# A memory-bound decode kernel: the small q-weight load moved to the front, and the engines' programs emitted without a block

## The chip, the cores and the metric

The kernel runs on one core of one Trainium2 chip. The metric is the device time of one execution in microseconds (us). Each execution also has a *span*, from the first to the last instruction that the profile shows on the core. The device time is longer than the span by 1.2 to 2.1 us in the runs here, and that difference is a main character of this study. It is called "the time outside the span" below.

## The reference, cut to what matters

One decode step of a transformer layer, batch 4, one token each, model width 576, all inputs bf16:

```python
x  = A_x                                        # [4, 1, 576]
h  = x + attention(layernorm(x))                # 32 query heads, 16 kv heads, head size 128
h2 = h + (relu(hn @ W_gate) * (hn @ W_up)) @ W_down   # hn = layernorm(h), inner width 4608
# attention:
q = x @ wq                                      # wq: [576, 4096], 4.7 MB
k = k_cache[:, :, -4096:, :]                    # the last 4096 positions: 67 MB
v = v_cache[:, :, -4096:, :]                    # 67 MB
o = softmax(q @ k.T * 128**-0.5) @ v;  return o @ wo
```

The caches and weights make 159.58 MB to be read once; the output is 4.6 KB.

## The kernel before

The program is first written as a list of operations for each engine, with the operations that each waits for. `emit` turns that into instructions and semaphore waits. Before, this happens inside a block: each engine's program is a body of its own, and when the block closes, all engines meet at a barrier (in the profile before, SP waits 0.2 us there for PE's sequencer).

```python
# in Prog.emit
        block = es.enter_context(nc.Block())

        def run(engine, e):
            seen = {}
            for o in self.q[e]:
                ...                              # waits on semaphores, then the instruction
        for e in ENGS:
            getattr(block, e)(lambda engine, e=e: run(engine, e))
```

All large loads are issued by SP on one queue, in the order of this code. The weights with 576 rows are loaded in two parts: rows 0 to 511 with four rows (32 KB) on each of the 128 partitions, and the last 64 rows with half a row (4 KB) on each.

```python
        s = ring_slot()                          # one of four 4 MB slots
        place(("wq", 0), wq_off, TILE, "QMM",    # 4 MB: rows 0..511
              lambda e: e.dma_start(out=arena[:, wq_off:wq_off + TILE], in_=main_rows(A_wq)), key=f"slot{s}")
        P.dma("sync", ("L", "wq", 1), lambda e: e.dma_start(out=pT[:, 0:2048], in_=last_rows(A_wq)), "d_wq1")   # 0.5 MB
        for g in range(NTILE):                   # 16 K tiles and 16 V tiles of 4 MB
            add_kv("K", g)
            if g >= 4:
                add_kv("V", g - 4)
        ...                                      # wo, W_gate, W_up, W_down
            for r0, r1 in ((0, 9),) if j < 3 else ((0, 6), (6, 8), (8, 9)):   # the last W_down load is cut in three
```

The tensor engine multiplies with the main q rows first and with the last 64 rows at the end. Each K tile is transposed by DVE before the tensor engine uses it. The end of the program:

```python
        for n in range(2):                       # the output, one half from SP, one from ACT
            P.dma(("sync", "scalar")[n], ("O", n), ..., "d_out", [f"OUT{n}"])
        P.op("sync", None, None, [("O", n) for n in range(2)])    # SP waits for both
        P.emit(nc, es)
```

## Time and profile before

| what | value | seen in |
|---|---|---|
| device time, first three runs | 379.36, 380.56, 380.57 us | times |
| span of the profiled run | 378.6 us | page |
| its device time less its span | 380.66 - 378.6 = 2.1 us | times and page |
| HBM bytes | 159.58 MB | page |
| load queue's share of the 16 DMA engines' time | 98.3% | page, part 3 |
| PE, DVE busy | 56%, 60% | page, part 1 |

The page of the kernel before: the span, each engine's busy time, then busy tenths of the DMA engines and GB/s in forty slices of the span, and the load queue with its packets, MB and share.

```profile
span 378.6 us, 2587 instructions
...
PE 213.2 (56%) x1471; PEld 37.6 (10%) x703; DVE 225.6 (60%) x164; ACT 54.4 (14%) x85; POOL 10.6 (3%) x29
...
DMA  8999999999999999999999999999999999999994
GB/s 333 440 443 429 409 435 443 443 429 409 435 443 440 427 414 433 443 436 426 419 435 443 429 426 426 435 433 436 429 422 435 436 429 429 448 413 421 418 423 183
...
q1 hardware_dynamic: 6632, 159.59, 98.3%
```

Only the first and the last slice have slack: the kernel is one long stream. By the packet records of this trace, from the first load packet (1.84 us) to the end of the last (374.64) it is 159.58 MB in 372.80 us, 428 GB/s. (A single slice shows up to 448, because the view counts a whole packet in the slice in which it starts; with each packet's bytes spread over its duration, the same records give 423 to 433 in every slice but the first and the last.)

The start, from the timeline (start in us, duration in us, engine, line, operation; in brackets the engine's idle time before it and what ended that). SPq is the issue of a DMA by SP.

```profile
0.80 0.40 SPq L256 DMA_DIRECT2D sb_arena<-in_A_wq_dram  x1
1.26 0.41 SPq L257 DMA_DIRECT2D sb_pp<-in_A_wq_dram  x1
...
13.28 0.62 PE L384 MATMUL psb<-sb_arena,sb_xnT 128*32 128x512 bf16 x4 [4.68 <-DMA sb_arena<-in_A_wq_dram]
...
24.24 8.71 DVE L427 STREAM_TRANSPOSE sb_arena<-sb_arena 128x8192 f32<-128x8192 f32 x1 [2.29 <-DMA sb_arena<-in_A_k_cache_dram]
...
33.00 0.65 PE L451 MATMUL psb<-sb_arena 128*32 128x512 bf16 x4 [12.46 <-DVE sb_arena L427]
```

The q matmuls wait for their load until 13.28, the first K tile is there at 24.24, and the first QK matmul follows at 33.00.

The tensor engine at the end (two batches of W_down matmuls), and then what SP waited for last:

```profile
371.93 1.28 PE L707 MATMUL psb<-sb_arena,sb_pp 128*32 128x288 bf16 x18 [1.83 <-DMA sb_arena<-in_B_W_down_dram]
373.98 2.35 PE L707 MATMUL psb<-sb_arena,sb_pp 128*32 128x288 bf16 x18 [0.77 <-DMA sb_arena<-in_B_W_down_dram]
```

```profile
SPq L136 <- DMA out_dram<-sb_out_sb: 1.0, 1, 1.0
...
SPq L136 <- PEq L136: 0.2, 1, 0.2
```

Eighteen matmuls took 1.28 us, and eighteen equal ones 2.35. Line 136 is where the block closes: SP waits 1.0 us for the output, then 0.2 for the barrier.

### The profile page before, as it was taken

To read this page: it belongs to the slowest core of one execution; us is meant where nothing else is said; L and a number is where in the kernel's file an instruction comes from. 1 tells how busy PE (TensorE), PEld (TensorE's weight loads), DVE (VectorE), ACT (ScalarE), POOL (GpSimd) and SP (SyncE) were. 2 spreads that over 40 slices of the span, in tenths; PEclk is the share of its full clock that TensorE was granted. 3 is DMA by queue.
4 is the path that set the end of the run, shared out by engine and by line. 5 is a ranking of instruction groups with operands and counts; after the bars stand their busy time and mean duration, and the time that the engine had idled before them with its cause. 6 is when DMAs were issued, how large, how long until landed. Compare 5 with 4: busy or idle time off the path is not lost.

```text
span 378.6 us, 2587 instructions
## 1 busy us (share of the span) xinstructions
PE 213.2 (56%) x1471; PEld 37.6 (10%) x703; DVE 225.6 (60%) x164; ACT 54.4 (14%) x85; POOL 10.6 (3%) x29
## 2 busy tenths in 40 slices
PE   0404442239919091749292835573746697885764
PEld 0000000001001010101010100010100011002422
DVE  3178878779392959593848777666658513334120
ACT  3192000211010114010101140101010501113010
POOL 8200000000000000000000000000000000000000
PEclk9966866659969788697888796989686978998697
DMA  8999999999999999999999999999999999999994
GB/s 333 440 443 429 409 435 443 443 429 409 435 443 440 427 414 433 443 436 426 419 435 443 429 426 426 435 433 436 429 422 435 436 429 429 448 413 421 418 423 183
DMA packets 6659, 159.74 MB, mean 422 GB/s; under 512 B 749, under 2 KB 889, under 8 KB 1529
## 3 DMA queue, kind: packets, MB, share of 16 engines
q1 hardware_dynamic: 6632, 159.59, 98.3%
q8 instruction: 8, 0.13, 0.1%
q14 instruction: 3, 0.02, 0.0%
q10 hardware_dynamic: 16, 0.01, 0.0%
HBM read 159.58 MB, written 0.00 MB: 422 GB/s over the span
## 4 chain that ended last, share of the span: by engine, by line
DMA 56%; PE 22%; DVE 20%; issue 0%; SPq 0%; ACT 0%
DMA sb_arena<-in_A_k_cache_dram 48%; DVE sb_arena L427 16%; PE psb L34 13%; DMA sb_arena<-in_B_W_down_dram 8%; PE psb L451 4%; PE psb L512 3%; DVE sb_o_tmp L525 1%; DVE sb_pp L490 1%; PE psb L707 1%; PE psb L478 1%; DVE sb_pp L473 0%; DVE sb_hx L456 0%; ACT sb_pp L470 0%; SPq L286 0%; DVE sb_out_sb L710 0%
## 5 line engine op out<-in xcount | busy, mean ns | idle before, releaser
L427 DVE STREAM_TRANSPOSE sb_arena<-sb_arena 128x8192 f32<-128x8192 f32 (+1 forms) x19 | 139.9, 7365 | 67.5 <-DMA sb_arena<-in_A_k_cache_dram 67.5
L451 PE MATMUL psb<-sb_arena 128*32 128x512 bf16 x256 | 41.8, 627 | 120.3 <-DVE sb_arena L427 120.3
L34 PE MATMUL psb<-sb_arena,sb_pp 128*128 128x512 bf16 x384 | 108.3, 392 | 0.0
L512 PE MATMUL psb<-sb_arena,sb_pp 128*128 128x512 bf16 x128 | 50.9, 398 | 8.9 <-DVE sb_o_tmp L525 8.9
L522 ACT COPY sb_o_tmp<-psb 32x512 f32<-32x512 f32 x32 | 18.5, 578 | 181.4 <-PE psb L34 181.1
L34 PE MATMUL psb<-sb_arena 128*32 128x512 bf16 x256 | 43.4, 645 | 0.0
L525 DVE TENSOR_TENSOR sb_o_tmp<-psb,sb_fm 32x512 f32<-32x512 f32 x32 | 21.7, 678 | 18.6 <-PE psb L34 18.1
L451 PEld LDWEIGHTS psb<-sb_arena 128*32 128x32 bf16 x256 | 9.1, 119 | 162.9 <-DVE sb_arena L427 133.3
L512 PEld LDWEIGHTS psb<-sb_arena,sb_pp 128*128 128x128 bf16 x128 | 12.8, 100 | 116.6 <-issue 116.6
L529 DVE TENSOR_REDUCE sb_o_sel<-sb_o_tmp 128x128 f32<-128x512 f32 x16 | 17.7, 1105 | 0.5
L470 ACT ACTIVATE sb_pp<-psb,sb_hx 128x1024 bf16<-128x1024 f32 x4 | 4.5, 1114 | 80.7 <-DVE sb_hx L467 80.7
L490 DVE TENSOR_TENSOR sb_pp<-psb,sb_m 128x1024 bf16<-128x1024 f32 x8 | 9.3, 1207 | 4.8 <-PE psb L478 4.8
L485 ACT ACTIVATE sb_pp<-psb,sb_m 128x512 bf16<-128x512 f32 x16 | 9.7, 693 | 14.9 <-PE psb L478 14.9
L528 DVE TENSOR_TENSOR sb_o_tmp<-sb_o_tmp,sb_fm 64x512 f32<-64x512 f32 x16 | 11.0, 689 | 0.5
L418 ACT COPY sb_arena<-sb_q_keep 32x256 bf16<-32x256 bf16 x8 | 9.7, 1449 | 0.1
L707 PE MATMUL psb<-sb_arena,sb_pp 128*32 128x288 bf16 x72 | 6.2, 327 | 4.0 <-DMA sb_arena<-in_B_W_down_dram 4.0
L473 DVE STREAM_TRANSPOSE sb_pp<-sb_pp 128x1024 bf16<-128x1024 bf16 x4 | 5.0, 1245 | 5.1 <-ACT sb_pp L470 5.1
L478 PE MATMUL psb<-sb_pp,sb_to_v 128*32 128x256 bf16 x64 | 4.3, 401 | 6.3 <-DVE sb_pp L473 6.3
L404 DVE CAST sb_pp<-psb 128x512 bf16<-128x512 f32 x1 | 2.4, 2427 | 8.8 <-PE psb L384 8.8
L710 DVE CAST sb_out_sb<-psb 32x288 bf16<-32x288 f32 x1 | 0.4, 446 | 10.7 <-PE psb L707 10.7
L34 PE MATMUL psb<-sb_arena,sb_hnT 128*32 128x384 bf16 x80 | 6.4, 405 | 0.0
L456 DVE TENSOR_REDUCE sb_hx<-psb 128x1 f32<-128x1024 f32 x4 | 4.9, 1225 | 2.0 <-PE psb L34 2.0
(123 smaller groups left out, 81.2 us busy)
## 6 DMA issues: line engine op xcount, KB each, us to landing
sb_arena<-in_A_k_cache_dram SPq DMA_DIRECT2D x16, 4096.0 KB, 26.2
sb_arena<-in_A_v_cache_dram SPq DMA_DIRECT2D x16, 4096.0 KB, 28.5
sb_arena<-in_A_wo_dram SPq DMA_DIRECT2D x1, 4608.0 KB, 25.0
sb_arena<-in_B_W_gate_dram SPq DMA_DIRECT2D x1, 4608.0 KB, 26.5
sb_arena<-in_A_wq_dram SPq DMA_DIRECT2D x1, 4096.0 KB, 12.4
sb_arena<-in_B_W_down_dram SPq DMA_DIRECT2D x3, 1296.0 KB, 30.6
sb_arena<-in_B_W_up_dram SPq DMA_DIRECT2D x1, 3456.0 KB, 27.5
sb_arena<-in_B_W_up_dram SPq DMA_DIRECT2D x1, 1152.0 KB, 29.9
```

Of the source, the lines that this page charges most:

```text
L34: return e.add_instruction(mybir.InstMatmult(name=e.bass.get_next_instruction_name(), engine=mybir.EngineType.PE, ins=[e.lower_ap(rhs), e. ...
L418: act("QW", lambda e, i=i, q=q: e.copy(out=bass.AP(tensor=arena, offset=32 * i * AW + 2 * i + q, ap=[[AW, 32], [512, 16], [136, 4], [32, 4]]),
L427: dve(("TRA", g), lambda e: e.transpose(out=dst, in_=src), [("L", "K", g)] if lo == 0 else [])
L451: fn = lambda e, out_=out_, lhsT=lhsT, rhs=rhs, start=start, stop=stop: e.matmul(out_, lhsT=lhsT, rhs=rhs, start=start, stop=stop, skip_gr ...
L485: act(("EV", b, 0), lambda e, a=a: e.activation(out=bass.AP(tensor=pp, offset=2 * a, ap=[[PPW, 128], [8, 2], [32, 128], [1, 2]]), in_=bank ...
L490: dve(("EV", b, 1), lambda e, n=n: e.tensor_tensor(out=bass.AP(tensor=pp, offset=16 + 8 * n, ap=[[PPW, 128], [32, 128], [2, 4], [1, 2]]), ...
L512: fn = lambda e, lhsT=lhsT, rhs=rhs, k=k, j=j: e.matmul(bank[2 + j], lhsT=lhsT, rhs=rhs, start=(k == 0), stop=(k == 7), skip_group_check=True)
L522: act(("OSC", g), lambda e, j=j: e.copy(out=o_tmp[32 * j:32 * j + 32, 0:512], in_=bank[2 + j][32 * j:32 * j + 32, :]), [("PV", g), ("OSEL" ...
L525: dve(("OSD", g), lambda e, j=j: e.tensor_tensor(out=ot(32 * j, 32), in0=bank[2 + j][32 * j:32 * j + 32, :].rearrange("p (t d) -> p t d", ...
L528: dve(("OS", g), lambda e: e.tensor_tensor(out=ot(64, 64), in0=ot(64, 64), in1=fmb(64, 64), op=ALU.mult), [("OSC", g)])
L529: dve(("OSEL", g), lambda e: e.tensor_reduce(out=o_sel[:, qd, b, :], in_=o_tmp[:, 0:512].rearrange("p (t d) -> p d t", d=DH), axis=AX.X, o ...
L707: pe(("DOWN", n), lambda e, j=j, r=r, n=n, wv=wv: e.matmul(bank[n][32 * n:32 * n + 32, 0:288], lhsT=hhT[:, r * 128 + 32 * j:r * 128 + 32 * ...
```

## The change

Its intent: drop the block with its branches and closing barrier, since SP alone waits for the output and the engines need not meet; and put the small load of q weights in front, so that it is there when the main one lands.

```diff
-        block = es.enter_context(nc.Block())
-
...
         for e in ENGS:
-            getattr(block, e)(lambda engine, e=e: run(engine, e))
+            run(getattr(nc, e), e)
...
+        P.dma("sync", ("L", "wq", 1), lambda e: e.dma_start(out=pT[:, 0:2048], in_=last_rows(A_wq)), "d_wq1")
         s = ring_slot()
         wq_off = slot0 + s * TILE
         place(("wq", 0), wq_off, TILE, "QMM", ...)
-        P.dma("sync", ("L", "wq", 1), lambda e: e.dma_start(out=pT[:, 0:2048], in_=last_rows(A_wq)), "d_wq1")
```

## The prediction

> **What bounds the kernel now.** The input stream from HBM. The page counts 159.58 MB read in a 378.6 us span; the DMA engines are at 90% or more in every slice but the first and the last, and the load queue alone has 98.3% of their time. The first DMA is issued at 0.80, bytes move from about 1.8, and the last W_down piece lands at 373.98 (chain of waits): about 429 GB/s. [...] PE is 56% busy, DVE 60%; neither paces the middle. After the last landing comes a serial tail of 4.6 us: 18 W_down matmuls 2.35, the copy 0.45, the output's issue 0.34, its landing about 1.0 (SP's wait), and about 0.4 to the end of the span, of which 0.2 is SP's wait for PE's sequencer where the block closes.
>
> **What the change removes, adds, moves.**
> 1. The closing barrier: the last 0.2 to 0.4 us of the span, all on the chain. The wait for the output stays. I take away 0.3 us.
> 2. The block's entry. The constructor's barrier stays (SP waits 0.7 us there); the first DMA follows at most 0.1 us later. I take 0.05 us, on the chain because it shifts the stream.
> 3. The last 64 rows of the q weights (0.5 MB) go before the main 4 MB. Same bytes, queue and issue cost (0.40 and 0.41 us). At 0.43 MB per us the small piece takes 1.2 us: it lands near 4 us instead of 14.5, the main part near 14.5 instead of 13.28. PE used the small piece only at 16.67 and never waited for it; now the first q matmul starts 1.2 us later. The q chain, whose eight copies end at 30.9, ends near 32.1. The first QK matmuls start at 33.0 behind the first K transpose, which waits for K's landing at 24.2 and does not move. So the delay is swallowed, with 0.9 us left. The fourth K load waits for the q matmuls and is issued near 19 instead of 18, with some 10 MB still queued ahead: no gap in the stream.
>
> So of the 1.2 us shift nothing reaches the end, and some 0.35 us of barrier and entry do.
>
> **Prediction.** The runs before are 379.36, 380.56 and 380.57. I predict 379.9 us, range 378.7 to 380.9. Chances: faster by over 2% 0.01, within 2% 0.98, slower 0.01.
>
> **What would show it.** SP's last wait for PE's sequencer gone; the span's end 0.3 us or less after the output lands; first DMA issued at 0.7 to 0.8; small q piece landing near 4, first q matmul near 14.5; first K transpose still near 24.2, first QK matmul near 33.0; last W_down landing within 0.3 us of 373.9.
>
> **What would make it wrong.** (a) The last 18 matmuls ran at a granted clock of 0.50 and took 2.35 us, against 1.28 for as many at 1.00: another phase of the throttle moves the end by 1 us, more than the change. (b) The stream's rate varies by fractions of a per cent between runs, as large as the gain. (c) If the q copies end after the first K transpose, QK starts late, but the backlog absorbs it (loads land 26 us after issue, and take under 10). (d) Small first packets could start the stream earlier or later by tenths.

## More of the kernel before

All executions counted here are of the state "fast". Inside that state most kernels here have two modes about 1 us apart; they are called *short* and *long*, and what goes with them is one of the findings. Effects of a few tenths of a microsecond are compared between short runs alone.

## The result

The median of six runs is 377.93 us (377.82 to 378.96), beside 379.69 us for the kernel before (379.36 to 380.57, six runs). The ratio is 0.9956, with a 95% interval of 0.9938 to 0.9974. Ratios here are the mean time of one kernel's fast runs over that of the other's of the same rounds, so not quite the ratio of the medians quoted.

So the change is 1.7 us faster by the means (1.8 by the medians). It stays inside the 2% band, as forecast, but the time lies under the stated range, and the gain is some four to five times the 0.35 us that the prediction added up.

The page of the changed kernel, the same lines as above:

```profile
span 376.6 us, 2561 instructions
...
PE 208.2 (55%) x1456; PEld 38.0 (10%) x703; DVE 226.6 (60%) x164; ACT 54.3 (14%) x85; POOL 10.5 (3%) x29
...
DMA  8999999999999999999999999999999999999996
GB/s 335 446 446 425 409 446 446 425 418 439 444 421 428 429 444 428 421 432 446 428 423 428 446 425 432 420 446 425 435 421 446 423 432 425 442 419 422 435 415 259
...
q1 hardware_dynamic: 6632, 159.59, 98.8%
```

The span is 2.0 us shorter, but the device time of the same two executions differs by 380.66 - 377.82 = 2.84. The rest is outside the span: 377.82 - 376.6 = 1.2 us now, 2.1 before.

The start of the changed kernel:

```profile
0.80 0.40 SPq L251 DMA_DIRECT2D sb_pp<-in_A_wq_dram  x1
...
1.25 0.41 SPq L255 DMA_DIRECT2D sb_arena<-in_A_wq_dram  x1
...
14.12 0.62 PE L382 MATMUL psb<-sb_arena,sb_xnT 128*32 128x512 bf16 x4 [6.47 <-DMA sb_arena<-in_A_wq_dram]
...
23.80 8.71 DVE L425 STREAM_TRANSPOSE sb_arena<-sb_arena 128x8192 f32<-128x8192 f32 x1 [1.69 <-DMA sb_arena<-in_A_k_cache_dram]
...
32.56 0.66 PE L449 MATMUL psb<-sb_arena 128*32 128x512 bf16 x4 [11.86 <-DVE sb_arena L425]
```

The first issue has not moved (0.80), so leaving the block's entry away is worth nothing. But the first K tile is there 0.44 us earlier, although the same bytes go ahead of it. That size is of this pair of profiles: a second profile of the changed kernel (e15 below) has the transpose at 24.17, only 0.07 earlier. By the packet records, the stream now lasts 372.16 us from its first packet to its last, not 372.80. This is steadier: of the eleven kept profiles with the half megabyte in front and no pause, ten have 372.00 to 372.31 us (one, e11, 372.64); the three in the order of before (before, e2, e8) have 372.69 to 372.80.

The end of it, and SP's last waits:

```profile
371.27 1.28 PE L705 MATMUL psb<-sb_arena,sb_pp 128*32 128x288 bf16 x18 [1.82 <-DMA sb_arena<-in_B_W_down_dram]
373.32 1.37 PE L705 MATMUL psb<-sb_arena,sb_pp 128*32 128x288 bf16 x18 [0.77 <-DMA sb_arena<-in_B_W_down_dram]
```

```profile
SPq L110 <- DMA out_dram<-sb_out_sb: 1.0, 1, 1.0
SPq L730 <- PEq L730: 0.7, 1, 0.7
```

The barrier wait is gone (the line with 0.7 is the one at the program's start, which stays). The last eighteen matmuls took 1.37 us here and 2.35 there. That is the difference between the modes, not the change, as the runs show ("beside the experiments" means run in the same rounds):

| | short runs | long runs |
|---|---|---|
| before (44 runs beside the experiments) | 30, mean 379.48 | 14, mean 380.44 |
| changed (12 runs: the six above, and e15) | 7, mean 377.89 | 5, mean 378.88 |

The profile of before happened to be a long run and that of the changed kernel a short one. Of the 18 kept profiles three are long runs (before, e4, e5), and in just these three the clock of the last matmuls was 0.50; in the others it was 1.00. Between short runs the change is worth 379.48 - 377.89 = 1.59 us; it is this that the experiments have to explain.

### The profile page after: what moved, and what is told of

It is laid out like the page before. It is cut to its first block, busy times and chain, and to the rows that moved or that the text cites. A ratio compares the mean times of both kernels' runs of the same rounds, so it can differ in the third digit from the quotient of the medians.

```text
span 376.6 us, 2561 instructions
## 1 busy us (share of the span) xinstructions
PE 208.2 (55%) x1456; PEld 38.0 (10%) x703; DVE 226.6 (60%) x164; ACT 54.3 (14%) x85; POOL 10.5 (3%) x29
## 4 chain that ended last, share of the span: by engine, by line
DMA 56%; PE 22%; DVE 20%; issue 1%; SPq 0%; ACT 0%
DMA sb_arena<-in_A_k_cache_dram 48%; DVE sb_arena L425 16%; PE psb L34 13%; DMA sb_arena<-in_B_W_down_dram 9%; PE psb L449 4%; PE psb L510 3%; DVE sb_o_tmp L523 1%; DVE sb_pp L488 1%; PE psb L476 1%; PE psb L705 0%; DVE sb_pp L471 0%; DVE sb_hx L454 0%; ACT sb_pp L468 0%; SPq L284 0%; DVE sb_out_sb L708 0%
## 5 line engine op out<-in xcount | busy, mean ns | idle before, releaser
L449 PE MATMUL psb<-sb_arena 128*32 128x512 bf16 x256 | 44.6, 639 | 119.3 <-DVE sb_arena L425 119.3
L34 PE MATMUL psb<-sb_arena,sb_pp 128*128 128x512 bf16 x382 | 106.9, 388 | 2.8 <-issue 2.7
L510 PE MATMUL psb<-sb_arena,sb_pp 128*128 128x512 bf16 x115 | 44.8, 390 | 8.9 <-DVE sb_o_tmp L523 8.9
L34 PE MATMUL psb<-sb_arena 128*32 128x512 bf16 x256 | 45.5, 646 | 0.0
L449 PEld LDWEIGHTS psb<-sb_arena 128*32 128x32 bf16 x256 | 10.0, 118 | 162.0 <-DVE sb_arena L425 132.4
L705 PE MATMUL psb<-sb_arena,sb_pp 128*32 128x288 bf16 x72 | 5.2, 288 | 4.0 <-DMA sb_arena<-in_B_W_down_dram 4.0
```

The lines of the kernel that those rows point to most:

```text
L34: return e.add_instruction(mybir.InstMatmult(name=e.bass.get_next_instruction_name(), engine=mybir.EngineType.PE, ins=[e.lower_ap(rhs), e. ...
L449: fn = lambda e, out_=out_, lhsT=lhsT, rhs=rhs, start=start, stop=stop: e.matmul(out_, lhsT=lhsT, rhs=rhs, start=start, stop=stop, skip_gr ...
L510: fn = lambda e, lhsT=lhsT, rhs=rhs, k=k, j=j: e.matmul(bank[2 + j], lhsT=lhsT, rhs=rhs, start=(k == 0), stop=(k == 7), skip_group_check=True)
```

## The experiments

Theory A: two independent parts, the block's end (inside and outside the span) and the start of the stream. Rivals: all of it comes from the block (B), or all but the barrier's 0.35 us from the swap (C).

### e1: the swap alone

```diff
  (kernel before; block kept)
+        P.dma("sync", ("L", "wq", 1), ...)      # in front of the main part
         place(("wq", 0), ...)
-        P.dma("sync", ("L", "wq", 1), ...)
```

> Block kept, only the q pieces swapped. Theory A (the change is the sum of two independent parts: the load stream starts up better, 0.65 us; the block's end costs 0.35 us inside the span and 0.85 us between the span's end and the end of the timed run): 0.5 to 0.7 us under before, run time minus span still about 2.06, stream about 372.2 us from first to last load packet. Rival B (all of the 1.7 us comes from removing the block, and the stream's 0.65 us is noise or a consequence of it): same time as before within 0.2 us.

Measured: five runs of 379.01 to 379.25, all short, mean 379.12, so 0.36 us under the short runs of before. Outside the span it is 2.10 us, as before. The stream lasted 372.04 us, and the first K transpose started at 23.91. The gain in time is half of what the stream's length in the two profiles promised, but it is there: B falls.

### e2: the block removed, the order of before

```diff
  (changed kernel)
-        P.dma("sync", ("L", "wq", 1), ...)      # back behind the main part
         place(("wq", 0), ...)
+        P.dma("sync", ("L", "wq", 1), ...)
```

> Block removed, the q pieces in the order of before. Theory A: 1.0 to 1.2 us under before, run time minus span about 1.22, stream still about 372.8 us. Rival B: 1.7 us under before. Rival C (everything but the 0.35 us barrier is the swap): 0.3 us under before.

Measured: short runs at 378.15 to 378.37, mean 378.27, so 1.21 us under before; one long run. Outside the span: 1.26 us. The stream is as long as before, 372.69 us. C falls. The parts add up: 0.36 + 1.21 = 1.57, against 1.59 for both.

### e3 and e4: barrier, branches, or holding the engines?

The instruction records put 0.35 of the 1.21 us inside the span: in the profile before, SP's wait for the output ends at 378.23 and the barrier at 378.58; in the changed kernel SP's wait is the span's last instruction. The other 0.83 us (2.08 less 1.25) is outside. e3 puts a barrier back without a block:

```diff
  (changed kernel)
         for e in ENGS:
             run(getattr(nc, e), e)
+        nc.all_engine_barrier()
```

> The changed kernel with an explicit all-engine barrier at the very end, still no block and no branches. Theory A1 (a barrier holds the other engines back until the output has landed, so what each does after its program can't overlap the tail): run time minus span back to about 2.06, total 1.1 to 1.2 us over the changed kernel. Rival A2 (the branch out of the block costs the time after the span): run time minus span stays 1.22, total only 0.2 to 0.3 over the changed kernel.

SP's last waits in e3:

```profile
SPq L110 <- DMA out_dram<-sb_out_sb: 1.0, 1, 1.0
...
SPq L119 <- PEq L119: 0.2, 1, 0.2
```

e4 has neither barrier nor branch; all five engines wait for the output's semaphore:

```diff
  (changed kernel)
-        P.op("sync", None, None, [("O", n) for n in range(2)])
+        for e in ENGS:
+            P.op(e, None, None, [("O", n) for n in range(2)])
```

> The changed kernel, where all five engines, not SP alone, wait for the output's semaphore at the end; no barrier, no branch, no extra semaphore traffic. Theory A1: about 0.8 us over the changed kernel, run time minus span about 2.06. Rival A3 (the barrier's own instructions cost it): equal to the changed kernel within 0.15 us, run time minus span 1.22.

| run | short runs, mean us | outside the span, mean us |
|---|---|---|
| before | 379.48 | 2.08 |
| changed | 377.89 | 1.25 |
| e3, barrier, no block | 378.95 (4 of 6 runs) | 2.09 |
| e4, all engines wait | 378.68 (2 of 6 runs) | 1.98 |

The branches are acquitted of the time outside the span: with a barrier alone nearly all is back (1.06 of 1.21 us), and that time is that of before. Inside the span they may cost about 0.1 us: from the end of SP's wait for the output to the end of the barrier it is 0.35 us before and 0.26 in e3. And most of that needs no barrier at all: it is enough that all engines wait for the output (0.73 of the 0.83 us outside).

### e5, e6, e7, e11: which engine is held

In these four the wait for the output stands in one other engine's program, and SP's is dropped.

```diff
  (changed kernel; e5 "tensor", e6 "scalar", e7 "gpsimd", e11 "vector")
-        P.op("sync", None, None, [("O", n) for n in range(2)])
+        P.op("tensor", None, None, [("O", n) for n in range(2)])
```

> The changed kernel, but the wait for the output's semaphore stands at the end of the tensor engine's program and not of SP's; no other engine is held. If each engine has closing work of its own after its program, and it runs side by side on the five, run time minus span is the closing work of the held engine: SP's is 1.25 us (changed kernel), the longest of the five is 1.97 (all held). Theory A1 with unequal engines: one of the three runs e5 to e7 shows about 1.97, the others other values of 1.2 to 2.0. Rival A4 (the number of engines held matters, not which): every one of the three shows about 1.25.

> As e5, with the wait at the end of ACT's program. A1: its own value between 1.2 and 2.0 us after the span. Rival A4: about 1.25.

> As e5, with the wait at the end of the GpSimd engine's program. A1: its own value between 1.2 and 2.0 us after the span. Rival A4: about 1.25.

> As e5 to e7, with the wait at the end of the vector engine's program. Run time minus span was 1.25 for SP, 1.40 for ACT, 1.51 for PE, 1.80 for GpSimd, 1.97 for all five. If all five together cost no more than the slowest of them, the vector engine is the one at about 1.97; if holding more engines adds up, it shows less than 1.8.

| engine that waits for the output | outside the span, mean us |
|---|---|
| SP (changed kernel) | 1.25 |
| ACT (e6) | 1.40 |
| PE (e5) | 1.52 |
| DVE (e11) | 1.57 |
| GpSimd (e7) | 1.80 |
| all five (e4) | 1.98 |
| all five, and a barrier (e3) | 2.09 |

The values of one kernel's runs lie within 0.15 us of each other (the spans are recorded to 0.1 us), so PE and DVE are not told apart. In time these kernels are slower than the changed one by about as much: short runs of 378.15 us (ACT, 3 runs), 378.35 (PE, 1), 378.29 (DVE, 4) and 378.40 (GpSimd, 2), beside 377.89. So it matters which engine comes last (rival A4 falls), and also, if less, how many: all five cost 0.18 us more than the slowest alone, which e5's expectation had at one engine with 1.97. The reading, argued and not seen, is that each engine has closing work after its own program, which overlaps the kernel's tail if the engine is let go early. These runs show only the time outside the span, 1.25 us (SP) to 1.80 (GpSimd) by the engine that waits and 1.98 with all five. What it consists of lies outside the profile and was not seen.

### e8: is it the packet size of the first load?

The 0.4 us of the swap remain. By the packet records, the first sixteen load packets of the kernel before (32 KB each) took 1.77 us on the mean; the later ones of the same load take 1.21 (all after 10 us: 1.22). First theory: large packets make a slow start. e8 keeps the order of before and cuts the main load:

```diff
  (e2)
-        place(("wq", 0), wq_off, TILE, ...)              # 32 KB per partition
+        place(("wq", "a"), wq_off, 2048, ...)            # 4 KB per partition
+        place(("wq", 0), wq_off + 2048, TILE - 2048, ...)   # 28 KB per partition
```

> No block, the last 64 rows second as before; but the main 4 MB of the q weights are cut into a first DMA of 4 KB per partition and a second of 28 KB. Theory R1 (the first packets being 32 KB is what costs the start: the first sixteen took 1.9 us against 1.21 later): the stream is as short as in the changed kernel, about 372.1 us, and the time 0.35 to 0.5 us under e2, that is about 377.9. Rival R2 (what helps is which rows come first, their addresses or that the main part lands later): as e2, stream about 372.7, time about 378.3.

Measured: short runs 377.98 to 378.42, mean 378.19, so 0.08 under e2 and 0.30 over the changed kernel; two runs were long (379.10, 379.36); the stream lasted 372.70 us and the first K transpose started at 24.31, as in e2 (24.29). What the theory forecast did not come; why not is taken up below.

### e9: is it any small piece in front?

```diff
  (e2)
+        P.dma("sync", ("L", "wq", 2), ... out=pT[:, 0:512] ...)       # 1 KB per partition, 128 KB
         place(("wq", 0), ...)
-        P.dma("sync", ("L", "wq", 1), ... out=pT[:, 0:2048] ...)
+        P.dma("sync", ("L", "wq", 1), ... out=pT[:, 512:2048] ...)
```

> No block. Only a quarter of each of the last 64 rows' halves (1 KB per partition, 128 KB in all) goes first, then the main 4 MB, then the other three quarters. Theory R3 (what helps is that the slow first packets are met on a small piece whose rows lie close together, the order of the rest being free): first K load's last packet ends before 23.7 us and the stream takes about 372.1 to 372.3 us, as in the changed kernel; time of undisturbed runs about 377.9 to 378.0. Rival R2 (what helps is that all of the small piece precedes the main one): as e2, first K load at 23.85, stream 372.7, undisturbed runs about 378.25.

Measured: short runs at 378.59 to 378.97, mean 378.81: slower than e2 by 0.54 us, which neither side expected; two runs were long. First K transpose at 24.62, stream 373.10 us. The sixteen large packets behind the small piece were slow all the same, 1.71 us.

### e12, e13, e14: rows, dose, and the time since the issue

Three looks, read by their packet records. Their one run each took 378.37, 378.71 and 382.06 us (e14, some 4 us over the short runs of the changed kernel, as expected), beside 379.51 for one run of before.

```diff
  (e12: e2, K tile 0 in front of both q loads)
+        sq = P.q["sync"]
+        sq[0:3] = [sq[2], sq[0], sq[1]]
  (e13: as e9, with 2 KB per partition in front)
  (e14: changed kernel; the main q load is issued only after a memset of GpSimd)
+        P.q["sync"][1].deps.append("c_qW")
```

> No block; the first K load goes ahead of both q loads. If the slow first packets belong to the position (any 4 MB load of 32 KB packets that opens the stream), its first sixteen packets take about 1.8 us on the mean, the q load's then 1.21. If they belong to the rows of the q weights, the K packets take 1.21 and the q packets behind them 1.8.

> No block; 2 KB per partition of the last q rows (256 KB) ahead of the main part. If it is a matter of time (since stream start or issue), large packets that start before about 3.2 us after the span's start are slow and later ones are not: mean of the first sixteen between 1.35 and 1.6 us. If it is a matter of a small piece being whole in front: 1.7 as with 128 KB.

> The changed kernel, but SP issues the main q load only when GpSimd has finished a memset at about 5.8 us, so the stream runs dry for some 3.5 us and starts again. If a load's large packets are slow as long as they follow close on the load's own issue (here about 1 us), the first sixteen take about 1.8 us again. If they are slow only in the first 1.5 us of the whole stream, they take 1.2 to 1.3. The kernel as a whole should come out 3 to 4 us slower.

SP's issues in e14: the main q load goes out 5 us after the small one.

```profile
0.80 0.41 SPq L251 DMA_DIRECT2D sb_pp<-in_A_wq_dram  x1
5.86 0.33 SPq L255 DMA_DIRECT2D sb_arena<-in_A_wq_dram  x1
```

| kernel | small load in front | large load issued at | its first 16 packets start at | mean duration of these, us |
|---|---|---|---|---|
| before | none | 0.80 | 1.84 to 2.64 | 1.77 |
| e2 | none | 0.80 | 1.82 to 2.48 | 1.86 |
| e12 (a K tile) | none | 0.80 | 2.21 to 2.86 | 1.68 |
| e9 | 128 KB | 1.25 | 2.39 to 3.56 | 1.71 |
| e13 | 256 KB | 1.27 | 2.85 to 3.82 | 1.41 |
| changed | 512 KB | 1.25 | 3.31 to 4.02 | 1.26 |
| e14 | 512 KB, then a pause | 5.86 | 6.82 to 8.22 | 1.89 |

It is not the rows: a K tile in front is slow too (e12). It is not the first microseconds of the program: in e14 the stream had begun 5 us before, and the load was as slow as ever (1.89 us). Two readings remain. One is how soon a load's large packets follow its own issue: about 1 us after it they take 1.7 to 1.9 us instead of 1.21, 2 us after it hardly more than 1.21, and e13 lies between. The other is how long the DMA engines have been at work without a pause: e14's queue had run dry (0 GB/s from 4.8 to 6.8 us), so its large packets start a stream anew, and in e9, e13 and the changed kernel they begin 0.6, 1.0 and 1.5 us after the stream's first packet and get faster in that order. In these kernels the two go together, and no run here separates them. In the kernel before, the sixteen DMA engines pay 1.77 - 1.21 = 0.56 us there. In the changed one, behind the half megabyte, they pay 1.26 - 1.21 = 0.05; the small packets have a start of their own to pay (the first sixteen took 0.37 us, later ones 0.16, so 0.21). As an estimate from these numbers, 0.56 - 0.05 - 0.21 = 0.30 us is left; 0.36 was measured in time.

Counting the bytes of the packet records checks this. The first 4.7 MB (all q weights) were in at 13.57 us in the kernel before and 13.61 in e2, and at 13.43 in e1, 13.36 and 13.45 in the two profiles of the changed kernel: 0.1 to 0.25 us earlier. In the pair of profiles shown, the lead is still 0.22 us at 157 MB (367.04 against 367.26) and becomes 0.67 only within the last 2.6 MB, where the DMA engines end one after another (from 371 us on, their busy share by microseconds is 0.98, 0.74, 0.50 and 0.08 in the kernel before, 0.99, 0.74, 0.43 and 0.00 in the changed one). So the start accounts for about 0.2 us of the 0.36; why the last bytes gain more is not shown.

Why the first large packets are slow, these runs do not show. The same byte count places the two misses. e9 has its first 4.7 MB at 14.02, so 0.41 of its 0.54 us behind e2 are lost at the start: its large packets paid the full price, behind small ones, and did not start on all sixteen engines until 3.56. e8 has them at 13.74. Its 28 KB packets came 2.3 us after their issue or later, and were near full speed at once (mean 1.16, later 1.08), but the cut costs as much as that saves: its first sixteen 4 KB packets took 0.51 us on the mean (0.37 in the changed kernel), and later 28 KB and 4 KB take 1.08 + 0.16 = 1.24 instead of 1.21. Added up over both q loads, the packets took 11.68 us for each of the sixteen engines in e8, 11.65 in e2 and 11.36 in the changed kernel. So e8 had no gain to show, and it does not tell whether the size of the first packets matters.

### e10, e15, e16: the two modes, and a better version

The windows view shows PE's granted clock at the end (start and end of the window and its length; busy us and instructions of PE, PEld, DVE, ACT, POOL; PEclk, DMA share, GB/s). First the kernel before, then the changed one:

```profile
373.00:374.00 1.00, 0.23 (x6) 0.02 (x4) 0.00 (x0) 0.00 (x0) 0.00 (x0) 0.68 0.50 189
374.00:375.00 1.00, 1.00 (x10) 0.67 (x12) 0.00 (x0) 0.00 (x0) 0.00 (x0) 0.50 0.08 30
```

```profile
373.00:374.00 1.00, 0.68 (x12) 0.52 (x12) 0.00 (x0) 0.00 (x0) 0.00 (x0) 1.00 0.43 158
374.00:375.00 1.00, 0.69 (x10) 0.21 (x6) 0.28 (x1) 0.24 (x1) 0.00 (x0) 1.00 0.00 0
```

The last eighteen matmuls met a clock of 0.50 in one and 1.00 in the other; e5, another long run, has the same 2.35 us at 0.50. Twelve of the eighteen wait for one piece of six rows. e10 cuts that piece, so that six can start earlier:

```diff
  (changed kernel)
-            for r0, r1 in ((0, 9),) if j < 3 else ((0, 6), (6, 8), (8, 9)):
+            for r0, r1 in ((0, 9),) if j < 3 else ((0, 3), (3, 6), (6, 8), (8, 9)):
...
-                        if r == 0 or (j == 3 and r in (6, 8)):
+                        if r == 0 or (j == 3 and r in (3, 6, 8)):
```

> The changed kernel with the last W_down load's first six rows cut into three and three, so that the tensor engine can start on it about 1 us earlier. Some runs of every kernel are about 1.05 us longer; I think that these are the ones whose last 18 matmuls meet a granted clock of 0.50 (2.35 us against 1.37 in the profiles). If so, the long mode comes down by 0.5 to 0.8 us, to about 378.2, and the short mode stays at 377.9 within 0.1. Rival (the two modes are not the tail's): both modes stay, 1.05 us apart.

> Short runs at 377.8 to 378.0, and of six runs one to three long ones at 378.8 to 379.0.

> If the long mode is the tail's clock: no run over 378.5. If it is not: one to three of six at 378.8 to 379.0, as for the changed kernel.

The tensor engine's last batches in e10: the first three rows' six matmuls have joined the batch before, and the rest comes in two sixes, the last after a wait of 0.17 us for its load.

```profile
371.33 1.65 PE L705 MATMUL psb<-sb_arena,sb_pp 128*32 128x288 bf16 x24 [1.84 <-DMA sb_arena<-in_B_W_down_dram]
373.44 0.55 PE L705 MATMUL psb<-sb_arena,sb_pp 128*32 128x288 bf16 x6 [0.47 <-DMA sb_arena<-in_B_W_down_dram]
374.16 0.66 PE L705 MATMUL psb<-sb_arena,sb_pp 128*32 128x288 bf16 x6 [0.17 <-DMA sb_arena<-in_B_W_down_dram]
```

Measured: all ten runs of e10 and e16 lie between 377.88 and 377.98. The changed kernel, on the same chip in the same rounds as e16, had three short runs (377.80 to 377.99) and three long ones (378.76 to 379.01). Five of twelve against none of ten: the long mode goes with the tail's shape, if on few runs (e1, with the old shape, also had none in five). The expectation had the long mode come down only to about 378.2; no run shows a second mode at all. How the cut does it is not shown. It need not be that it hides a halved clock: at half clock throughout, e4's last 36 matmuls took 4.50 us, and from e10's start at 371.33 that would end at 375.83, a microsecond after its 374.82. The clock records hint that the cut keeps the clock up instead. In the profiles of before, the changed kernel and e10 the clock changes only at times a multiple of 3.41 us apart (before, from 346 us on: at 346.05, 349.46, 352.88, 359.70 and 373.36; e10: at 352.27, 359.10 and 376.17). e5 and e10 had such a time at nearly the same place, 372.79 (where e5's clock changed) and 372.76 (3.41 before e10's 376.17); PE had been busy for 1.44 us of the 3.41 before it in e5 (1.43 in the kernel before, where it fell at 373.36) and for 1.57 in e10, and of these two only e5's clock fell:

```profile
373.00:374.00 1.00, 0.59 (x6) 0.42 (x8) 0.00 (x0) 0.00 (x0) 0.00 (x0) 0.50 0.50 184
```

```profile
373.00:374.00 1.00, 0.55 (x6) 0.21 (x6) 0.00 (x0) 0.00 (x0) 0.00 (x0) 1.00 0.52 192
```

That is the same window of e5, then of e10; it is one pair, and no proof. By the medians of e16's rounds e16 is the best version: 377.92 us, beside 378.37 for the changed kernel and 379.6 for the one before (ratio to before 0.9948, interval 0.9935 to 0.9962).

## Why the prediction was wrong

**Right.**
- The bound, and that the change stays inside 2%.
- The closing barrier inside the span: 0.3 us predicted, 0.35 found.
- The wait for SP at the barrier is gone, and the first DMA is still issued at 0.80; the entry's 0.05 us is nothing.
- The small piece in front lands near 4 us (its last packet ends at 4.02), and the q chain's delay is swallowed. It is even smaller than predicted: the eight copies end at 21.34 + 9.71 = 31.05 us, not near 32.1.
- The warning (a), that the last matmuls' granted clock moves the end by 1 us (18 of them took 2.35 us at 0.50, 1.28 at 1.00): these are the two modes. It makes single runs differ, but it is not why the median fell out of the range. The short runs of before were already at 379.3 to 379.7, and those of the changed kernel are 1.59 us lower.

**Wrong.** The sum "some 0.35 us of barrier and entry" had two terms mis-sized.

1. "The closing barrier: the last 0.2 to 0.4 us of the span, all on the chain." The mechanism was right, but the term was sized by what the span shows. The barrier also holds four engines back until the output has landed, and what they do after their programs (argued, not seen) then comes after it. What the runs show is 0.83 us outside the span (2.08 to 1.25; e2, e3 and e4). The term is 1.21 us in all. The hint was in the numbers of before: device time 380.66, span 378.6, and the prediction never asked what the other 2.1 us were.
2. "Same bytes, queue and issue cost ... So of the 1.2 us shift nothing reaches the end." The step from equal bytes to an equal stream failed. When a load opens the stream, its first large packets are slow (1.77 us instead of 1.21), and a small load in front bridges most of that (1.26); in the byte counts this is about 0.2 us, and the rest of the gain comes at the stream's end and stays open. The term was 0 and is 0.36 us (e1). The prediction's own check, the first K transpose "still near 24.2", failed by 0.44 us in the profile of the result (by 0.07 in e15). Its warning (d), that small first packets could start the stream earlier by tenths, named the place but not the means: the first packet starts at 1.81 instead of 1.84.

One misreading on the way: the prediction says that the last W_down piece lands at 373.98. The chain shows what releases the last eighteen matmuls there, the six-row piece; by the packet records the last piece's last packet ends at 374.64. It did not change the sum.

## What to carry to other kernels

When a kernel's tail is a wait for the output, let only one engine wait and let the others run out of their programs; here that was worth 0.83 us outside the span, and it mattered which engine waited (1.25 us outside the span with SP, 1.80 with GpSimd). For a kernel bound by its loads, look at the durations of the first packets: here the first large ones took 1.77 us with no small load in front, 1.71 behind 128 KB and 1.26 behind 512 KB, against 1.21 later. Before taking a difference of a microsecond for an effect, sort the runs into their modes. And try the last load cut more finely: here the long mode was gone with it in ten runs.
